# A planned kernel for attention and a squared-ReLU layer: late waits priced in the plan, and the first batch's weights made fourfold by TensorE

## The chip, the cores and the metric

The kernel runs on one core of a Trainium2 chip. The metric is the device time of one execution in microseconds (us). Engine names are those of the profile: PE is TensorE's matmuls, PEld its weight loads, DVE VectorE, ACT ScalarE, POOL GpSimd, SP the engine whose queue issues every DMA here.

## The reference

```python
def _attn_ref(x, inducing):            # x: 4 x 12480 x 128, inducing: 32 x 128
    scale = 1.0 / np.sqrt(C)
    def mab(q, kv):
        s = scale * (q @ kv.transpose(0, 2, 1))
        s = s - s.max(-1, keepdims=True)
        a = np.exp(s)
        a /= a.sum(-1, keepdims=True) + 1e-09
        return a @ kv
    h = mab(I, x)                      # 32 induced points a batch, over all 12480 tokens
    return mab(x, h)
def _moe_ref(x, w_in, w_out, s, b):    # x: 49920 x 128, w_in: 128 x 2048, w_out: 2048 x 128
    h = x @ w_in
    r = np.maximum(h, 0.0)
    g = s * (r * r) + b
    return g @ w_out
```

All of it is float32, but w_in and w_out, which come as float64. The layer runs on the attention's output.

## The kernel before

**What the bulk is.** A token's attention over 32 points and the layer's first product are folded into one: the 32 points' hT (channels by points) times w_in gives 32 x 2048 numbers, and a token's row of h is its 32 softmax weights times these. The product is taken at the fast float32r rate with both operands as a rounded high half and a low rest, so the contraction has 128 rows: `wst` holds the 32 rows four times (two copies of the high half in partitions 0 to 63, two of the low half in 64 to 127), and `a2t` holds the softmax weights as high, low, high, low. The layer's second product is split in the same way (`w_hi`, `w_lo`, and g1 with the rest g2).

Tokens go in blocks of 480, 26 blocks a batch, 104 in all. A block has 8 *pairs* (832 in all); a pair makes 256 of the 2048 rows of h by 2 matmuls (line 857), its ReLU on ACT or DVE (872, 874), its square on ACT (940) and the product h*r on DVE (895), the difference on POOL or DVE (917), and 6 matmuls into the block's output bank (965). The first NATIVE = 6 pairs are *native*: square on ACT (897) or DVE (899), and plain float32 matmuls with the unsplit `w_out_raw` (tile `wst` in line 965's rows). At a block's end line 973 or 975 adds the bias and SP writes the block out.

**Side work.** The attention of later batches runs as *visits* in the second output bank between a block's end and the next: `attend` (scores of 4 blocks against hT, a softmax on DVE and ACT, then `spread`: 4 DMAs a block write `a2t`), `scores`, `top`, `values`, `points` and `w_unit` (hT times w_in in 4 column groups, a high and a low half in `hl`, then `spread_w`: 4 DMAs for each of 4 quarters write `wst`).

**The opening.** The first batch has its own code. SP loads in the order of ORDER: x as channels by tokens in 7 groups of 4 blocks (13 pieces of 480 KB; groups 0 to 6), w_in and w_out as 64-bit words in 4 slices of 512 KB each, and x with tokens in partitions (`xQ`, pieces of 480 KB) for the groups in TURNED; the other groups are turned by PE transposes (line 428) and copies. `narrow` makes a slice float32 with 5 DVE and 2 ACT instructions (lines 307 to 324), `split_w_out` its halves (332, 334). `p1_unit` takes a group's scores (455), maximum, exp, transposes (475) and the sum of values (486); `h_unit`, `h_sums` and `h_out` join the groups into hT (line 575). Then `w_unit(0)` and `spread_w` make `wst`, and `attend_first` (line 779 to the copy into `a2t`) makes the first block's weights without DMAs; `attend(0, 0)` gives those of blocks 1 to 3. `keep_warm` fills PE with idle matmuls (1085) until the first `a2t` is there.

**What sets the order.** `Plan` runs all this as generators before anything is sent to the chip: each `yield` names an engine (or a choice of two), an estimated length and the events that it needs, and `Plan.run` is a list scheduler that emits the instruction whose (start time + WEIGHT x urgency) is least, with a filler rule (SLIP). Its output is the fixed order of each engine's instructions; the engines then wait for semaphores as the data demand. In the version before, every step that follows another becomes ready LAT = 0.1855 us after it, on whichever engine. `landing` estimates when a DMA ends.

Of the kernel before, what the change touches and what calls it, by code (L numbers as in the profile page):

```python
# [33 lines left out]
SLIP = 0.1677  # L34
WEIGHT = 0.0292
LEAN = {"ACT": -0.62, "DVE": -0.2727}
R_LEAN = {"DVE": -0.2236, "ACT": -0.2367}
# [4 lines left out]
SQ = 1.0679  # L42
MM = 0.2134
S_U = -1.7495
C_U = -10.3238
OUT_HI = 3.0192
# [3 lines left out]
SPREAD = -50.0  # L50
# [34 lines left out]
class Plan:  # L85
# [7 lines left out]
    def __init__(self):  # L93
        self.free, self.events, self.units, self.end, self.start = {}, {}, [], 0.0, 0.0

    def spawn(self, unit, urgency=0.0, ready=0.0):
        self._step(unit, urgency, ready)

    def _step(self, unit, urgency, ready=None):
        want = next(unit, None)  # L100
        if ready is None:
            ready = self.end + LAT
        if want is not None:
            eng, us, *waits = want
            if not isinstance(eng, dict):
                engs, lean = {eng: us}, LEAN
            elif isinstance(us, dict):
                engs, lean = eng, us
            else:
                engs, lean, waits = eng, LEAN, [us, *waits]  # L110
            more = sum(w for w in waits if isinstance(w, float))
            waits = [w for w in waits if not isinstance(w, float)]
            self.units.append((unit, urgency + more, ready, engs, waits, urgency, lean))
# [6 lines left out]
    def backlog(self, eng):  # L120

        ev = self.events
        return sum(u[3][eng] for u in self.units if eng in u[3] and u[2] <= self.end and all(w in ev for w in u[4]))

    def set(self, name):
        self.events[name] = self.end

    def run(self):
        ev = self.events
        while self.units:  # L130
            able = {}
            for u in self.units:
                _, urgency, ready, engs, waits, _, lean = u
                if any(w not in ev for w in waits):
                    continue
                ready = max([ready] + [ev[w] + LAT for w in waits])
                at, eng = min(
                    ((max(ready, self.free.get(e, 0.0)), e) for e in engs),
                    key=lambda x: x[0] + engs[x[1]] + lean.get(x[1], 0.0),
                )  # L140
# [12 lines left out]
            self._step(u[0], u[5])  # L153
# [3 lines left out]
def tile_attn_relu2(ctx: ExitStack, tc: tile.TileContext, xT, xN, xQ, indT, w_in, w_out, s_rep, b_rep, outT):  # L157
# [142 lines left out]
    def narrow(name, dst, *waits):  # L300
# [10 lines left out]
        yield "ACT", 0.5  # L311
        nc.scalar.activation(out=e, in_=e, func=AF.Relu, scale=8.0, bias=rebias)
        yield "ACT", 0.52
# [14 lines left out]
    def split_w_out(c):  # L328
        raw = w_out_raw
        sl = slice(c * (WC // P), (c + 1) * (WC // P))  # L330
        yield "ACT", 0.5, ("w_out", c)
        nc.scalar.copy(out=w_hi[:, sl, :], in_=raw[:, sl, :])
        yield "DVE", 0.6
        nc.vector.tensor_tensor(  # L334
            out=w_lo[:, sl, :], in0=raw[:, sl, :], in1=w_hi[:, sl, :].bitcast(F32), op=ALU.subtract
        )
        plan.set(("w_split", c))

    def bias_unit(ps, *waits):
# [9 lines left out]
        yield "ACT", 0.3  # L349
        sums = p2.tile([P, P], F32, name="s2", bufs=1)  # L350
        nc.scalar.activation(out=sums, in_=ps[:, 0:P], func=AF.Copy, scale=1.0 / M)
        yield "PE", 0.3
        nc.tensor.matmul(ps[:, 256:258], sums, ones[:, 0:2], start=True, stop=True)
        yield "DVE", 0.1
# [57 lines left out]
    def load_turned(g):  # L412
        for h in range(-(-blocks_in(g) // SB)):
            j = g * GR // SB + h
            yield "SP", 0.45, ("v done", j - 4)
            nc.sync.dma_start(out=home["q"][j % 4], in_=xQ[j])
            plan.events["turn", j] = landing(1.25)

    def turn_x(g, h, ps, *waits):

        j = g * GR // SB + h
        yield "PE", 0.87, *waits, ("x half", j), ("v done", j - 4)
# [7 lines left out]
        yield dict(ACT=0.9, DVE=1.14), 0.0  # L430
# [3 lines left out]
    def p1_unit(g, ps, *waits):  # L434
# [22 lines left out]
        yield "DVE", 0.69  # L457
# [3 lines left out]
        yield "DVE", 0.08  # L461
# [3 lines left out]
        yield "ACT", 0.75, *e_free  # L465
# [7 lines left out]
        yield "PE", 0.45  # L473
# [4 lines left out]
        yield dict(ACT=0.49, DVE=0.61), 0.0, *e_free  # L478
# [16 lines left out]
        yield dict(ACT=0.18, DVE=0.21), 0.0  # L495
# [3 lines left out]
    def common_max(m, ps):  # L499

        yield "PE", 0.07
        nc.tensor.transpose(ps[0:1, 0:P], m, ident)
        yield "DVE", 0.2
        r = sm.tile([1, 1, M], F32, name="mrow")
        nc.vector.reduce_max(out=r[:, 0, :], in_=ps[0:1, 0:P].rearrange("p (q i) -> p i q", q=NQ), axis=AX.X)
        yield "ACT", 0.25
        rq = sm.tile([1, NQ, M], F32, name="mrows", bufs=1)
        nc.scalar.mul(rq, r[:, 0:1, :].broadcast_to([1, NQ, M]), -scale)
        yield "PE", 0.11
        nc.tensor.matmul(ps[:, 128:129], rq.rearrange("p q i -> p (q i)"), ones[0:1, 0:1], start=True, stop=True)  # L510
        yield "DVE", 0.15

    def h_unit(b, ps, *waits):
        d = st[b]
        yield "DVE", 0.1, *waits
# [6 lines left out]
        yield "ACT", 0.2  # L522
# [19 lines left out]
    def h_sums(b, l, ps):  # L542

        d = st[b]
        yield "PE", 0.2
        ps = ps()
        nc.tensor.matmul(ps[:, 0:1], sel, l, start=True, stop=True)
        yield "DVE", 0.16
        rl = sm.tile([P, 1], F32, name="rl")
        nc.vector.tensor_scalar_add(rl, ps[:, 0:1], 1e-9)  # L550
        yield "DVE", 0.16
# [4 lines left out]
    def h_out(b, ps, *waits):  # L556
# [11 lines left out]
        yield "DVE", 0.35, ("rl", b)  # L568
        hg = p2.tile([P, P], F32, name="s2", bufs=1)
        nc.vector.tensor_scalar(out=hg, in0=ps[:, 0:P], scalar1=d["rl"], scalar2=None, op0=ALU.mult)  # L570
        yield "PE", 0.25
        nc.tensor.matmul(ps[:, 256:256 + P], hg, sel, start=True, stop=True)
        yield "DVE", 0.22
# [3 lines left out]
        plan.set(("hT", b))  # L577

    def w_unit(b, ps, *waits):
# [4 lines left out]
        yield "PE", 1.08, ("hT", b), *[("w_in", c) for c in range(nc_)], *waits  # L584
# [7 lines left out]
        yield dict(ACT=0.59, DVE=0.7), 0.0, *free  # L592
# [3 lines left out]
        yield "DVE", 0.7  # L596
        nc.vector.tensor_sub(out=hl[:, 1], in0=ps, in1=hl[:, 0].bitcast(F32))
        left = list(range(nc_))
        for c in range(nc_):
            plan.spawn(spread_w(b, c, hl, n, left), SPREAD + c, plan.end + LAT)  # L600

    def spread_w(b, c, hl, n, left):
        yield "SP", 2.4 if b else 1.6
# [9 lines left out]
        plan.events["wst", b, c] = landing(0.8) if b else landing(0.3, 1.7)  # L613
# [4 lines left out]
    def scores(b, g, ps, *waits):  # L618
# [15 lines left out]
        yield "PE", 1.04, ("x", b, g, 1), *waits  # L634
# [5 lines left out]
        yield "DVE", 0.65  # L640
        nc.vector.reduce_max(out=d["mx"][0:rows, g:g + 1], in_=ps[0:rows, 0:BLK], axis=AX.X)
        yield dict(ACT=0.56, DVE=0.65), 0.0
# [3 lines left out]
    def top(b, ps, *waits):  # L646

        d = st[b]
        yield "DVE", 0.16, *[("scores", b, g) for g in range(NG)], *waits
# [9 lines left out]
    def values(b, g0, ps, *waits):  # L659
# [4 lines left out]
        for g in gs:  # L664
            rows = M * blocks_in(g)
            e = d["s"][0:rows, g]
            yield "ACT", 0.8, ("top", b), *waits
# [4 lines left out]
            yield "DVE", 0.66, *e_free  # L672
# [4 lines left out]
        yield "PE", 0.1 + 0.83 * len(gs), *[("xn", b, g, half) for g in gs for half in range(-(-TB // TH))], *waits  # L677
# [13 lines left out]
        yield "DVE", 0.29  # L691
# [7 lines left out]
    def points(b, ps, *waits):  # L699

        d = st[b]
        yield "DVE", 0.16, *[("p1", b, g) for g in range(NG)], *waits
# [3 lines left out]
        yield "PE", 0.11  # L706
        nc.tensor.matmul(ps[:, 0:1], sel, l, start=True, stop=True)
        yield "DVE", 0.15
        rl = sm.tile([P, 1], F32, name="rl")
        nc.vector.tensor_scalar_add(rl, ps[:, 0:1], 1e-9)  # L710
        yield "DVE", 0.16
        nc.vector.reciprocal(out=rl, in_=rl)
        yield "ACT", 0.35
        hg = p2.tile([P, P], F32, name="s2", bufs=1)
        nc.scalar.mul(hg, d["acc"], rl)
        yield "PE", 0.25
        nc.tensor.matmul(ps[:, 256:256 + P], hg, sel, start=True, stop=True)
        yield "DVE", 0.28
# [8 lines left out]
    def attend(b, g, ps, *waits):  # L727
        nb = blocks_in(g)
        rows = M * nb
        yield "PE", 1.04, ("hT", b), ("x", b, g, 2), *waits  # L730
# [34 lines left out]
        yield "DVE", 0.66  # L765
# [4 lines left out]
        for q in mine:  # L770
            plan.spawn(spread(b, g, q), SPREAD, plan.end + LAT)

    def attend_first(ps):
# [10 lines left out]
        yield "DVE", 0.28  # L784
        mx = sm.tile([P, TB], F32, name="mx2")[0:T, 0:NQ]
        nc.vector.reduce_max(out=mx, in_=v, axis=AX.X)
        yield "DVE", 0.28
        nc.vector.tensor_tensor(out=v, in0=v, in1=mx.unsqueeze(2).broadcast_to([T, NQ, M]), op=ALU.subtract)
        yield "ACT", 0.28
        nc.scalar.activation(out=v, in_=v, func=AF.Exp, scale=scale)  # L790
        yield "DVE", 0.28
        nc.vector.reduce_sum(out=sums, in_=v, axis=AX.X)
        yield "DVE", 0.16
        nc.vector.tensor_scalar_add(sums, sums, 1e-9)
        yield "DVE", 0.18
        l = sm.tile([P, TB], F32, name="l2")[0:T, 0:NQ]
        nc.vector.reciprocal(out=l, in_=sums)
        yield "DVE", 0.28
        nc.vector.tensor_tensor(out=v, in0=v, in1=l.unsqueeze(2).broadcast_to([T, NQ, M]), op=ALU.mult)
        yield dict(ACT=0.38, DVE=0.43), 0.0  # L800
# [4 lines left out]
        yield "DVE", 0.43  # L805
        nc.vector.tensor_tensor(out=A[:, :, :, 1, :], in0=vr, in1=A[:, :, :, 0, :].bitcast(F32), op=ALU.subtract)
        n, free = ring_in_order("a2t", 3)
        yield "PE", 0.5
# [3 lines left out]
        yield dict(ACT=0.57, DVE=0.66), 0.0, *free  # L812
# [7 lines left out]
    def spread(b, g, q):  # L820

        turn, free = ring_in_order("a2t", 3)
        yield "SP", 2.4 if b or g else 1.6, *free, ("hl", b, g)
# [22 lines left out]
    def pair(k):  # L846
# [4 lines left out]
        yield "PE", 2 * MM, M_U, free, ("a2t", b, blk), ("wst", b, 2 * pr * P // WC), ("mm1", k - 1)  # L851
# [32 lines left out]
        else:  # L884
            q["R"].append((n, plan.end))
            if len(q["R"]) == 1:
                plan.spawn(square(k - n), k + SQ, plan.end + LAT)
# [18 lines left out]
        if kind == "N":  # L906
            ops = [(w_out_raw[:, 2 * pr + u, :], g[:, u, :]) for u in range(2)]
            plan.spawn(out_part(k, ops, 1.6, "w_out", lambda: plan.set(("g", g_turn))), k + OUT, plan.end + LAT)
# [12 lines left out]
        plan.spawn(out_part(k, ops, 2 * MM, "w_split", lambda: plan.set(("g2", n2))), k + OUT, plan.end + LAT)  # L921
# [6 lines left out]
    def square(k0):  # L928
# [3 lines left out]
        done = [n for n, us in q["R"] if us + LAT <= plan.start + 0.01]  # L932
# [8 lines left out]
        for i in range(lo, hi):  # L941
# [4 lines left out]
                out_part(k0 + i, ops, 4 * MM, "w_split", lambda: g1_used(q)), k0 + i + OUT_HI, plan.end + LAT  # L946
            )
        if q["R"]:
            plan.spawn(square(k0), k0 + 1 + SQ, q["R"][0][1] + LAT)
# [99 lines left out]
    def w_work():  # L1049
        yield from w_unit(0, lambda: hs[1][:, 0])  # L1050
        plan.set(("h", 1))
        plan.set(("h", 2))

    def opening():
# [17 lines left out]
        for at, f, args in loads:  # L1072
            yield from f([("ob", at - 1)] if at else [], *args)
# [20 lines left out]
    def after():  # L1094
# [4 lines left out]
        plan.spawn(w_work(), FIRST + W_URGENCY)  # L1099
# [52 lines left out]
```

## Time and profile before

| | |
|---|---|
| median of 3 runs | 1579.77 us (1578.29 to 1580.2) |
| the profiled execution's own time | 1579.85 us |
| its span | 1578.1 us |
| PE, DVE, ACT, POOL busy | 1559.3, 1462.8, 1504.9, 1479.3 us |
| granted TensorE clock, mean | 0.998 |
| DMA | 132.17 MB, mean 84 GB/s |

The span is what the trace covers from its first instruction to its last; the profiled execution's own time is 1.8 us longer. Matmuls are pipelined, so PE's busy time includes overlap, and a stretch in which PE is shown as busy throughout may still hold short stalls. A row's "idle before" is the time that an engine did nothing just ahead of those instructions, with what ended it.

### The profile page before, as it was taken

To read this page: it belongs to the slowest core of one execution; us is meant where nothing else is said; L and a number is where in the kernel's file an instruction comes from. 1 tells how busy PE (TensorE), PEld (TensorE's weight loads), DVE (VectorE), ACT (ScalarE), POOL (GpSimd) and SP (SyncE) were. 2 spreads that over 40 slices of the span, in tenths; PEclk is the share of its full clock that TensorE was granted. 3 is DMA by queue.
4 is the path that set the end of the run, shared out by engine and by line. 5 is a ranking of instruction groups with operands and counts; after the bars stand their busy time and mean duration, and the time that the engine had idled before them with its cause. 6 is when DMAs were issued, how large, how long until landed. Compare 5 with 4: busy or idle time off the path is not lost.

```text
span 1578.1 us, 24618 instructions
## 1 busy us (share of the span) xinstructions
PE 1559.3 (99%) x8140; PEld 1288.6 (82%) x8140; DVE 1462.8 (93%) x1580; ACT 1504.9 (95%) x1780; POOL 1479.3 (94%) x668
## 2 busy tenths in 40 slices
PE   8799999999999999999999999999999999999999
PEld 5478888888888888888788788888888888888887
DVE  5899999999999989999999999999999999999997
ACT  5799999999999999999999999999999999999998
POOL 0299999999999999999999999999999999999998
PEclk9999999999999999999999999999999999999999
DMA  9332224212133233221223322322222112112110
GB/s 319 97 113 87 90 88 150 64 51 90 38 107 119 73 122 119 73 73 56 76 66 101 111 78 100 120 82 63 79 59 66 39 51 70 32 51 70 53 33 23
DMA packets 54522, 132.17 MB, mean 84 GB/s; under 512 B 11548, under 2 KB 38044, under 8 KB 54396
## 3 DMA queue, kind: packets, MB, share of 16 engines
q1 hardware_dynamic: 54396, 130.59, 26.1%
q8 instruction: 66, 1.08, 0.3%
q14 instruction: 60, 0.49, 0.1%
HBM read 75.48 MB, written 25.56 MB: 64 GB/s over the span
## 4 chain that ended last, share of the span: by engine, by line
PE 96%; DVE 1%; DMA 1%; SPq 1%; ACT 0%; issue 0%; ACTq 0%; DVEq 0%
PE x L965 67%; PE h L857 23%; PE x L735 2%; PE x L683 1%; PE x L638 1%; DMA xn<-in_xQ_dram 1%; PE h L428 0%; SPq L606 0%; DVE w_lo L334 0%; PE x L486 0%; DMA wst<-hl 0%; DMA xt<-in_xT_dram 0%; PE x L588 0%; PE x L455 0%; DVE g L895 0%
## 5 line engine op out<-in xcount | busy, mean ns | idle before, releaser
L917 POOL TENSOR_TENSOR g<-g,g 128x960 fp32r<-128x960 f32 x660 | 1478.1, 2286 | 93.3 <-ACT g L940 73.3
L965 PE MATMUL x<-g,w_hi 128*128 128x480 f32 x3304 | 1062.1, 375 | 0.0
L940 ACT ACTIVATE g<-r 128x960 fp32r<-128x960 f32 (+1 forms) x812 | 796.6, 1020 | 16.2 <-DVE r L874 5.1
L895 DVE SCALAR_TENSOR_TENSOR g<-h,r 128x960 f32<-128x960 f32 x660 | 743.4, 1147 | 34.7 <-ACT r L872 26.8
L965 PEld LDWEIGHTS x<-g,w_hi 128*128 128x128 f32 x3304 | 618.2, 187 | 88.4 <-POOL g L917 1.7
L872 ACT ACTIVATE r<-h 128x960 f32<-128x960 f32 x673 | 634.3, 968 | 19.3 <-PE h L857 14.6
L965 PE MATMUL x<-g,w_lo 128*128 128x480 f32 x1652 | 619.8, 375 | 2.9 <-DVE w_lo L334 2.9
L857 PE MATMUL h<-a2t,wst 128*128 128x480 f32 x1664 | 500.3, 382 | 5.1 <-DMA wst<-hl 4.1
L857 PEld LDWEIGHTS h<-a2t,wst 128*128 128x128 f32 x1664 | 300.1, 187 | 97.9 <-issue 38.9
L965 PEld LDWEIGHTS x<-g,w_lo 128*128 128x128 f32 x1652 | 309.6, 187 | 51.9 <-issue 5.5
L917 DVE TENSOR_TENSOR g<-h,g 128x960 fp32r<-128x960 f32 x166 | 191.6, 1154 | 17.6 <-ACT g L940 8.1
L895 DVE SCALAR_TENSOR_TENSOR h<-h,r 128x960 f32<-128x960 f32 x166 | 192.2, 1158 | 6.6 <-ACT r L872 6.3
L874 DVE TENSOR_SCALAR r<-h 128x960 f32<-128x960 f32 x159 | 182.9, 1150 | 9.3 <-PE h L857 7.7
L973 ACT ACTIVATE ob<-x,bias,s_sb 128x480 f32<-128x480 f32 x101 | 75.6, 749 | 10.8 <-PE x L965 10.2
L735 PE MATMUL x<-xt,hT 128*32 128x480 f32 x208 | 28.3, 578 | 0.0
L766 DVE TENSOR_TENSOR hl<-x,hl 128x480 fp32r<-128x480 f32 (+1 forms) x28 | 18.4, 657 | 8.1 <-ACT hl L188 7.2
L638 PE MATMUL x<-xt,ind_sb 128*32 128x480 f32 x156 | 21.2, 578 | 0.0
L741 DVE STREAM_TRANSPOSE x<-x 128x480 f32<-128x480 f32 (+1 forms) x28 | 19.3, 689 | 1.5 <-PE x L735 1.4
L683 PE MATMUL x<-xn,eT 128*32 128x128 f32 (+1 forms) x630 | 20.7, 274 | 0.0
L683 PEld LDWEIGHTS x<-xn,eT 128*32 128x32 f32 (+1 forms) x630 | 17.5, 109 | 3.9 <-issue 2.3
L759 DVE STREAM_TRANSPOSE x<-x 128x480 f32<-128x480 f32 (+1 forms) x28 | 19.5, 697 | 1.0
L750 DVE TENSOR_REDUCE x<-x 128x15 f32<-128x480 f32 (+1 forms) x28 | 18.4, 659 | 1.4 <-ACT x L748 1.0
(149 smaller groups left out, 368.7 us busy)
## 6 DMA issues: line engine op xcount, KB each, us to landing
xt<-in_xT_dram SPq DMA_DIRECT2D x41, 960.0 KB, 5.1
out_dram<-ob SPq DMA_DIRECT2D x104, 240.0 KB, 2.0
a2t<-hl SPq DMA_DIRECT2D x412, 60.0 KB, 2.0
xn<-in_xN_dram SPq DMA_DIRECT2D x18, 512.0 KB, 4.7
xn<-in_xN_dram SPq DMA_DIRECT2D x18, 448.0 KB, 5.7
xt<-in_xT_dram SPq DMA_DIRECT2D x13, 480.0 KB, 4.3
wst<-hl SPq DMA_DIRECT2D x64, 64.0 KB, 2.0
r<-in_xT_dram SPq DMA_DIRECT2D x7, 480.0 KB, 8.8
```

The lines of the kernel that those rows point to most:

```text
L638: nc.tensor.matmul(ps[M * q:M * (q + 1), 0:BLK], ind_sb, xt[:, q], start=True, stop=True)
L683: nc.tensor.matmul(ps[M * c:M * (c + 1), 0:P], eT[0:rows, n], xn_tiles[b, g, half][0][0:rows, n - half * TH], start=m < P // M, stop=m + P ...
L735: nc.tensor.matmul(ps[M * q:M * (q + 1), 0:BLK], hT[:, 0:M], xt[:, q], start=True, stop=True)
L759: nc.vector.transpose(out=s, in_=s)
L857: nc.tensor.matmul(h[:, u, 0:BLK], wst[:, c * P:(c + 1) * P], A, start=True, stop=True)
L872: nc.scalar.activation(out=r, in_=hv, func=AF.Relu)
L874: nc.vector.tensor_scalar(out=r, in0=hv, scalar1=0.0, scalar2=None, op0=ALU.max)
L895: nc.vector.scalar_tensor_tensor(out=g, in0=hv, scalar=0.0, in1=r, op0=ALU.max, op1=ALU.mult)
L917: eng.tensor_tensor(out=g2, in0=g, in1=hi.bitcast(F32), op=ALU.subtract)
L940: nc.scalar.activation(out=q["g1_t"][:, sl, :], in_=q["r_t"][:, sl, :], func=AF.Square)
L965: nc.tensor.matmul(o, w, g, start=first and n == 0, stop=left == 0 and n == len(ops) - 1)
L973: nc.scalar.activation(out=ob, in_=o, func=AF.Identity, bias=bias, scale=s_sb)
```

## The change

- **The plan's prices.** A step's delay after the one that releases it now depends on both engines: none on PE, 0.15 us on DVE, 0.175 on ACT when the same engine did the earlier step, else LAT plus the waker's share (0.1 for PE, 0.03 DVE, 0.015 ACT, 0.03 POOL). Nearly all estimated lengths are replaced (a DVE step of a visit 0.57 instead of 0.65, PE's visits about 0.1 longer). Eleven or so urgencies and SLIP, WEIGHT move, most a little.
- **Fourfold weights.** `w_first` takes the place of `w_unit(0)` and its DMAs: hT has its 32 columns four times already, so 4 full float32 matmuls (128 columns of weights, 512 columns each) give all four copies at once; a copy rounds them into `wst`, and a DVE subtraction turns partitions 64 to 127 into the low rest.
- **The opening's loads.** Group 4 is turned by PE too (TURNED is 5 alone: two pieces of xQ fewer); two slices of w_out move ahead of x 2 and x 4, the order of w_in moves; a row of `xQ` in HBM is 48 floats (192 bytes) longer.
- **Later loads wait.** The x loads that stand ahead of block 0 (for the first visits) are planned after the `a2t` of block 1 has landed instead of at once.
- NATIVE is 5; a pair's first matmuls no longer name the pair before as an event (their order stays: a pair is spawned by the one before).

The core of the diff (lengths alone left out):

```diff
 LAT = 0.1855
-SLIP = 0.1677
-WEIGHT = 0.0292
+WAKE = {"PE": 0.1, "DVE": 0.03, "ACT": 0.015, "Pool": 0.03, "SP": 0.0}
+SAME = {"PE": 0.0, "DVE": 0.15, "ACT": 0.175, "Pool": 0.1, "SP": 0.0}
+SLIP = 0.1757
+WEIGHT = 0.0234
-R_LEAN = {"DVE": -0.2236, "ACT": -0.2367}
+R_LEAN = {"DVE": -0.2236, "ACT": -0.2106}
-SQ = 1.0679
+SQ = 1.3068
-S_U = -1.7495
+S_U = -2.6693
-OUT_HI = 3.0192
+OUT_HI = 3.1
-SPLIT_U = 11.22
-NATIVE = 6
-H_U = -5.8
-N_U = -2.41
-W_IN_U = -200.15
-W_OUT_U = 0.21
+SPLIT_U = 9.84
+NATIVE = 5
+H_U = -73.92
+N_U = -0.27
+W_IN_U = -194.01
+W_OUT_U = 0.92
+W_STEP = 1.0
-TURNED = (4, 5)
+TURNED = (5,)
+Q_PAD = 48
 ORDER = (
-    ("x", 0), ("x", 1), ("w_in", 0), ("x", 2), ("x", 3), ("w_in", 1), ("x", 4), ("w_in", 2), ("x", 5),
-    ("w_in", 3), ("x", 6), ("q", 4), ("q", 5), ("w_out", 0), ("w_out", 1), ("w_out", 2), ("w_out", 3),
+    ("x", 0), ("x", 1), ("w_out", 0), ("x", 2), ("w_in", 0), ("x", 3), ("w_out", 1), ("x", 4), ("w_in", 1),
+    ("w_in", 2), ("x", 5), ("x", 6), ("w_in", 3), ("q", 5), ("w_out", 2), ("w_out", 3),
 )
...
+    def lag(self, src, e):
+        return SAME[e] if src == e else LAT + WAKE[e]
+    def ready(self, u):
...
+        return {
+            e: max([at + self.lag(src, e) if at else 0.0] + [ev[w] + self.lag(self.by.get(w), e) for w in u[4]])
+            for e in u[3]
+        }
...
-            nc.sync.dma_start(out=home["q"][j % 4], in_=xQ[j])
-            plan.events["turn", j] = landing(1.25)
+            nc.sync.dma_start(out=home["q"][j % 4], in_=xQ[j, :, 0:SB * NQ * P])
+            plan.events["turn", j] = landing(2.1)
...
+    def w_first(c, ps, done):
+        yield "PE", 0.95, ("hT", 0), ("w_in", c)
...
+        sl = slice(c * WC, (c + 1) * WC)
+        ps = ps()
+        nc.tensor.matmul(ps, d["hT"], w_in_sb[:, sl], start=True, stop=True)
+        yield dict(ACT=0.48, DVE=0.6), 0.0
+        copy(d["wst"][:, sl], ps)
+        yield "DVE", 0.6
+        lo = d["wst"][P // 2:P, sl]
+        nc.vector.tensor_sub(out=lo, in0=ps[P // 2:P], in1=lo.bitcast(F32))
+        plan.set(("wst", 0, c))
...
-        yield "PE", 2 * MM, M_U, free, ("a2t", b, blk), ("wst", b, 2 * pr * P // WC), ("mm1", k - 1)
+        yield "PE", 2 * MM, M_U, free, ("a2t", b, blk), ("wst", b, 2 * pr * P // WC)
...
-            yield from f([("ob", at - 1)] if at else [], *args)
+            yield from f([("ob", at - 1) if at else ("a2t", 0, 1)], *args)
...
-        plan.spawn(w_work(), FIRST + W_URGENCY)
+        for c in range(F // WC):
+            plan.spawn(w_work(c), FIRST + W_URGENCY + W_STEP * c)
```

More of the change, by code (lines that the diff above doesn't have):

```diff
@@ L112, in _step @@
             waits = [w for w in waits if not isinstance(w, float)]
-            self.units.append((unit, urgency + more, ready, engs, waits, urgency, lean))
+            self.units.append([unit, urgency + more, (ready, src), engs, waits, urgency, lean, None])
     def extend(self, us):
@@ L118, in extend @@
         self.free[self.eng] = self.end
-    def backlog(self, eng):
-        ev = self.events
-        return sum(u[3][eng] for u in self.units if eng in u[3] and u[2] <= self.end and all(w in ev for w in u[4]))
     def set(self, name):
         self.events[name] = self.end
+        self.by[name] = self.eng
+    def lag(self, src, e):
+        return SAME[e] if src == e else LAT + WAKE[e]
+    def ready(self, u):
+        ev, (at, src) = self.events, u[2]
+        for w in u[4]:
+            if w not in ev:
+                return None
+        return {
+            e: max([at + self.lag(src, e) if at else 0.0] + [ev[w] + self.lag(self.by.get(w), e) for w in u[4]])
+            for e in u[3]
+        }
     def run(self):
-        ev = self.events
         while self.units:
@@ L132, in run @@
             for u in self.units:
-                _, urgency, ready, engs, waits, _, lean = u
-                if any(w not in ev for w in waits):
+                if u[7] is None:
+                    u[7] = self.ready(u)
+                if u[7] is None:
                     continue
-                ready = max([ready] + [ev[w] + LAT for w in waits])
+                urgency, engs, lean = u[1], u[3], u[6]
                 at, eng = min(
-                    ((max(ready, self.free.get(e, 0.0)), e) for e in engs),
+                    ((max(at, self.free.get(e, 0.0)), e) for e, at in u[7].items()),
                     key=lambda x: x[0] + engs[x[1]] + lean.get(x[1], 0.0),
@@ L429, in turn_x @@
         x_used(g, h)
-        yield dict(ACT=0.9, DVE=1.14), 0.0
+        yield dict(ACT=0.85, DVE=1.05), 0.0
         copy(t.rearrange("p a q c -> p a (q c)"), ps[0:T])
@@ L577, in h_out @@
         plan.set(("hT", b))
+    def w_first(c, ps, done):
+        yield "PE", 0.95, ("hT", 0), ("w_in", c)
+        d = st[0]
+        if "wst" not in d:
+            d["wst"] = wst_pool.tile([P, F], F32R, name="wst")
+        sl = slice(c * WC, (c + 1) * WC)
[7 more added lines that the diff above has]
+        plan.set(("wst", 0, c))
+        for name in done:
+            plan.set(name)
     def w_unit(b, ps, *waits):
@@ L583, in w_unit @@
         nc_ = F // WC
-        yield "PE", 1.08, ("hT", b), *[("w_in", c) for c in range(nc_)], *waits
+        yield "PE", 1.19, ("hT", b), *[("w_in", c) for c in range(nc_)], *waits
         d["wst"] = wst_pool.tile([P, F], F32R, name="wst")
@@ L612, in spread_w @@
             plan.set(("hl", n))
-        plan.events["wst", b, c] = landing(0.8) if b else landing(0.3, 1.7)
+        plan.events["wst", b, c] = landing(0.8)
     def scores(b, g, ps, *waits):
@@ L648, in top @@
         d = st[b]
-        yield "DVE", 0.16, *[("scores", b, g) for g in range(NG)], *waits
+        yield "DVE", 0.09, *[("scores", b, g) for g in range(NG)], *waits
         ps = ps()
@@ L666, in values @@
             e = d["s"][0:rows, g]
-            yield "ACT", 0.8, ("top", b), *waits
+            yield "ACT", 0.68, ("top", b), *waits
             nc.scalar.activation(
@@ L676, in values @@
             eTs[g] = eT, e_turn, rows
-        yield "PE", 0.1 + 0.83 * len(gs), *[("xn", b, g, half) for g in gs for half in range(-(-TB // TH))], *waits
+        yield "PE", 0.19 + 0.9 * len(gs), *[("xn", b, g, half) for g in gs for half in range(-(-TB // TH))], *waits
         ps = ps()
@@ L701, in points @@
         d = st[b]
-        yield "DVE", 0.16, *[("p1", b, g) for g in range(NG)], *waits
+        yield "DVE", 0.09, *[("p1", b, g) for g in range(NG)], *waits
         ps = ps()
@@ L886, in pair @@
             if len(q["R"]) == 1:
-                plan.spawn(square(k - n), k + SQ, plan.end + LAT)
+                plan.spawn(square(k - n), k + SQ, plan.end)
             yield "DVE", 1.065, S_U
@@ L931, in square @@
         yield "ACT", 0.893, *([] if "g1_t" in q else [q["g1"][1]])
-        done = [n for n, us in q["R"] if us + LAT <= plan.start + 0.01]
+        done = [n for n, us in q["R"] if us + LAT <= plan.start + 0.02]
         lo, hi = done[0], done[-1] + 1
@@ L1047, in tile_attn_relu2, with w_work @@
     before = [-2, -1, *turns]
[L1049 to L1052, printed above, removed]
+    def w_work(c):
+        yield from w_first(c, lambda: hs[1 + c // 2][:, c % 2], [("h", 1 + c // 2)] if c % 2 else [])
     def opening():
```

164 lines of the change are left out of this document (83 added, 81 removed).

## The prediction

> **What bounds the kernel now.** I read the page first (busy times, chain), then how many matmuls fall into a stretch, then the opening by stages, by the chain and by the waits. The page:
>
> ```profile
> span 1578.1 us, 24618 instructions
> PE 1559.3 (99%) x8140; PEld 1288.6 (82%) x8140; DVE 1462.8 (93%) x1580; ACT 1504.9 (95%) x1780; POOL 1479.3 (94%) x668
> PE 96%; DVE 1%; DMA 1%; SPq 1%; ACT 0%; issue 0%; ACTq 0%; DVEq 0%
> ```
>
> PE is the bound, and the chain that ended last is PE for 96%. Since a busy PE can hide stalls, I count. First the pace: two timeline rows of PE with 29 matmuls of 480 columns from the one's start to the other's; a native product; two visits.
>
> ```profile
> 299.76 0.59 PE L857 MATMUL h<-a2t,wst 128*128 128x480 f32 x2
> 305.95 0.37 PE L965 MATMUL x<-g,w_hi 128*128 128x480 f32 x1
> ...
> 60.57 1.77 PE L965 MATMUL x<-g,wst 128*128 128x480 f32 x4
> ...
> 80.04 1.01 PE L638 MATMUL x<-xt,ind_sb 128*32 128x480 f32 x8
> ...
> 235.06 1.94 PE L683 MATMUL x<-xn,eT 128*32 128x128 f32 x60
> ```
>
> (305.95 - 299.76) / 29 = 0.213 us a matmul; a native pair's 4 stand 0.40 apart (1.77 less one of 0.57, by 3), so 1.6 us; a visit of 8 takes 1.0, one of 60 takes 1.9. Then the counts of line 965 and, below, line 857, before and after 100 us:
>
> ```profile
> 49.50:100.00 50.50, 31.02 (x107) 20.03 (x108) 1.00 0.38 118
> 100.00:1574.00 1474.00, 1171.47 (x4874) 911.23 (x4873) 1.00 0.24 77
> ...
> 49.50:100.00 50.50, 15.46 (x50) 8.56 (x50) 1.00 0.38 118
> 100.00:1574.00 1474.00, 484.85 (x1614) 291.59 (x1614) 1.00 0.24 77
> ```
>
> From 100 us on: 6488 matmuls x 0.2134 = 1384.5 us, and by the code 46 visits of `attend` and `scores` x 1.0, values worth 10.5 x 1.9 and some 6 of small matmuls: about 72. That leaves some 17 us of 1474 in which PE stalls (1.1%). From 49.5 to 100: 24 native matmuls x 0.40, 133 others x 0.213, and 2.5 of side work make 40.5 of 50.5 us, a loss of about 10. Before 49.5 PE does no pair at all. So the time is: start of the first pair, plus 1498 us of work that no part of the change but NATIVE touches, plus about 27 us of stalls, plus 4 at the end. The change can gain in the first and in the stalls. The opening by stages (PE, PEld, DVE, ACT, POOL busy, granted clock, DMA share and GB/s):
>
> ```profile
> 20.00:30.00 10.00, 8.00 (x109) 4.46 (x106) 8.99 (x21) 7.95 (x18) 0.00 (x0) 1.00 0.98 304
> 30.00:40.00 10.00, 8.63 (x97) 6.62 (x97) 3.16 (x11) 3.65 (x9) 0.00 (x0) 0.66 0.89 278
> ...
> 45.00:50.00 5.00, 4.21 (x26) 2.67 (x26) 4.93 (x13) 2.63 (x6) 0.00 (x0) 1.00 0.29 70
> 50.00:60.00 10.00, 5.92 (x20) 3.13 (x18) 9.86 (x18) 9.94 (x13) 0.00 (x0) 1.00 0.75 218
> ```
>
> To 40 us it is DMA (share 0.9 to 1.0) while DVE and ACT have room; from 45 to 60 DVE is full. The chain names the transfer:
>
> ```profile
> 23.83 7.92 DMA xn<-in_xQ_dram
> ...
> 31.79 1.92 PE x L486 x28
> ...
> 34.84 1.89 PE h L428 x8
> ...
> 38.81 1.02 PE h L486 x16
> ...
> 42.57 0.20 DVE hT L575
> ...
> 55.57 4.37 DMA wst<-hl
> ```
>
> **The change, part by part.**
>
> *A. When hT is ready.* What ends last is `xQ`. Its four issues and their times to landing, and the DMA rate with x and weights in the queue (first row) and with `xQ` in it (second):
>
> ```profile
> L416 SPq DMA_DIRECT2D xn<-in_xQ_dram x4: 325/338/402, 23.3 to 26.2; - x4
> DMA to landing us min/median/max: 6.3/8.0/9.7
> ...
> 12.00:22.00 10.00, 8.90 (x123) 6.35 (x121) 7.28 (x15) 7.72 (x17) 0.00 (x0) 1.00 1.03 416
> 26.00:34.00 8.00, 5.69 (x56) 2.91 (x49) 6.06 (x14) 4.93 (x13) 0.00 (x0) 0.84 1.01 241
> ```
>
> They land from 29.6 (23.3 + 6.3) to 35.9 (26.2 + 9.7), 2.1 us apart, at 241 GB/s against 416 for the rest. After: two pieces fewer are -4.2; two slices of w_out now stand ahead, 524 kB each at 416 GB/s, +2.5. The last piece lands at 34.2. What follows it before is 6.9 us, to 42.77; of that, group 6's turn (1.89) and its values (1.02) need no longer wait behind group 4's `xQ` and are done earlier. From the end of line 486 at 39.8 to hT it is 3.0; before that come group 5's values, between 1.0 (full clock) and 1.9 (these rows, at half): 4.0 to 4.9, I take 4.5, so hT at 38.7, **4.0 us earlier**. Bounds: nothing earlier than 2 (group 4's transposes, two turning copies and part of two narrowed slices now fall into 20 to 30, where DVE has 10% left) and 6 if the longer rows of `xQ` load at the other pieces' pace, 1.2 instead of 2.1, twice.
>
> The Trainium skill's "DMA: Bandwidth & Descriptors", section "Latency and other measured facts", has that padding a large row pitch by 192 B did not restore the rate while 4 KiB did; that pitch was 4 MiB, and nothing here shows this one. Its section on why a DMA increments its semaphore by 16 lets 120 rows use only 15 engines, padded or not. By both the pieces stay at 2.1 and the sum as it is; with a pad that works it would be 1.7 less.
>
> *B. From hT to the first pair.* Before it is 49.57 - 42.77 = 6.8 us:
>
> ```profile
> 45.53 0.69 DVE L597 TENSOR_TENSOR hl<-h,hl 128x512 fp32r<-128x512 f32 x1
> ...
> 47.62 0.53 PE L811 MATMUL x<-accb,hl 120*128 120x120 f32 x4 [0.79 <-DVE hl L806]
> 48.19 0.56 ACT L188 CAST a2t<-x 128x480 fp32r<-128x480 f32 x1 [1.14 <-PE x L811]
> 49.57 1.13 PE L857 MATMUL h<-a2t,wst 128*128 128x480 f32 x4
> ```
>
> That is `attend_first`, which stays. `w_first` is 4 float32 products of 512 columns: by the native row (0.40 a pass of 480, two passes) 0.86 each, 3.4 us of PE, in time that idle matmuls fill now. It has 4 copies instead of one (about 0.6 on ACT) and 4 subtractions instead of one, 4 x 0.69: +2.1 on DVE. Against that, half of w_out's narrowing (5 DVE instructions of 512 columns a slice, at most 0.69 each by line 597's row, so 5 to 7 us for two slices, an estimate) leaves the full stretch for the time before 40. The first quarter of `wst` is ready some 1.0 + 0.9 + 0.6 + 0.7 and 0.6 of hand-overs after hT, 3.8, less than 6.8. So B stays: 0, between -1 and +1.2. The 16 `wst` DMAs go; what is late next is the `a2t` copy at 48.75. If that cover went, line 857 would wait on the later quarters, 0.9 us apart.
>
> *C. Stalls up to 100 us*, about 10 now. The rows that name them, with the subtractions of `split_w_out` and the two ACT steps of a native pair:
>
> ```profile
> PE h L857 <- DMA wst<-hl: 4.1, 2, 2.7
> PE x L965 <- DVE w_lo L334: 2.9, 1, 2.9
> ...
> 59.57 0.68 DVE L334 TENSOR_TENSOR w_lo<-wst,w_hi 128x512 fp32r<-128x512 f32 x1
> ...
> 67.97 5.58 DVE L334 TENSOR_TENSOR w_lo<-wst,w_hi 128x512 fp32r<-128x512 f32 x3 [0.40 <-ACT w_hi L332]
> ...
> L872 ACT ACTIVATE r<-h 128x960 f32<-128x960 f32 x10 | 9.5, 961 | 2.2 <-PE h L857 2.2
> L897 ACT ACTIVATE g<-r 128x960 f32<-128x960 f32 x5 | 4.9, 1004 | 0.1
> ```
>
> Of the 4.1 the shorter wait, 1.4, falls where PE has no product ready anyway (pair 0's square is not done), so 2.7 goes. The `w_lo` stall of 2.9 stands behind three subtractions that took 1.9 each on average beside POOL's first work, where the first, at 59.57 with POOL idle, took 0.68; with two slices narrowed, and so split, before the pairs begin I let 2.0 go. Late next is ACT: a native pair costs it 0.96 + 1.00 (lines 872, 897) against 2.03 on PE, and narrowing and splitting come on top; 0.5 lost. Sum **-4.2**, bounds -1 (DVE still has the softmax of `attend(0, 0)`, splits and two slices to do, and sets the pace) and -7 (both named waits go whole). The loads that wait have the other block writes behind them on SP and the visits from block 1 or 2 on waiting for them; a block is 64 matmuls x 0.213 = 13.7 us, so they have that long to land. Nothing lost.
>
> *D. NATIVE 5:* 4 x 0.40 = 1.6 of PE become 6 x 0.213 = 1.28: **-0.3**.
>
> *E. The order from 100 us on.* Weight loads of line 857 that came late, 100 to 1574, and a pair's first product behind one (0.67, while those at 299.76 took 0.59):
>
> ```profile
> PEld h L857 <- issue: 34.1, 71, 0.8
> PEld h L857 <- DVE g L895: 10.2, 33, 0.8
> PEld h L857 <- DVE r L874: 3.9, 5, 0.8
> ...
> 76.89 0.67 PE L857 MATMUL h<-a2t,wst 128*128 128x480 f32 x2
> ```
>
> 109 late loads x 0.08 = 9 of the 17 us. The new plan charges PE 0.1 after any other engine's step, so where another product is ready it is put first. The trace of before can't show the new order. Bounds: -9 (all go) and +9 (as many new ones, from shorter visit steps that make the plan promise more than DVE keeps); I take a quarter of the gain, **-2.5**, since the order was already within 1.1% of the work.
>
> Sum: -4.0 + 0 - 4.2 - 0.3 - 2.5 = -11.0 us against the profiled execution's 1579.85 (span and 1.8 around it), 0.08 above the median of the runs: 1568.8.
>
> **The rivals.**
>
> 1. *The start moves, the stalls don't go:* DVE has the same work between hT and the first `a2t` of block 1 and only shifts. For it: DVE at 99% from 45 to 60. Against it: 5 to 7 us of narrowing leave, 2.1 come. A and D alone: 1575.5.
> 2. *The clock.* The 30 to 40 row has 0.66, after a stretch in which PE waited for `xQ`. If it is at half for `w_first`, its 3.4 us become 6.9 and `attend_first`'s transposes stand behind them on PE: up to 3.4 later, 1572.3. Against it: group 4's wait is gone, and PE has idle matmuls to run from the last group on. The Trainium skill's "TensorE: Matmul & The Clock Gate", Part 1, says that PE drops to half after an idle window of about 3.4 us and needs as long a busy one to return. By that rule the wait for the last `xQ` piece is just such a window; the 0.66 agrees.
> 3. *The order is much better:* stalls after 100 us halve, -8 instead of -2.5: 1563.3.
> 4. *Slower: the order is worse.* The place is line 857 behind 895 and 872: with visit steps planned 0.08 shorter, DVE's h*r comes later than planned and PE waits. A loses nothing, but stalls from 100 us on must grow by 8.5 + 3.2 = 11.7, from 17 to 29, for the kernel to be slower by 0.2%; doubled to 34 it gives 1579.85 - 8.5 + 17 = 1588.4. Against it: the order is within 1.1% of the work already with one price for every wait, and PE's own wait, which decides, becomes dearer in the plan.
> 5. *The change does not do what it says:* the planner lets DVE take the two early w_out slices ahead of the turning copies, SP waits for a buffer of theirs with x 5, x 6 and `xQ` queued behind, and hT is not earlier; only C, D, E remain: 1572.8.
>
> **How the numbers follow.** The forecast with A to E near their middle has 0.50, rival 1 0.13, 2 0.09, 3 0.15, 4 0.07, 5 0.06. The likeliest one's own range is 1563 to 1574, from A's and C's bounds. The range goes to 1559 below (rival 3 with A at 6) and 1576.5 above (rival 1). A measurement of this kernel tells about 0.2%, 3.2 us, from no change. Faster by more (under 1576.6): the forecast, 2, 3, 5 and most of 1, 0.89; within it: the rest of 1 and some of 4, 0.06; slower: 0.05.
>
> **What would show it.** A: line 575 at 38 to 40 us and the two `xQ` pieces 2.1 apart. B: line 857 first at 44 to 47, no `wst` DMA before the second batch, 4 products of `w_first` 0.9 apart (1.8 if rival 2 holds). C: the waits on `wst` gone, that on `w_lo` under 1. E: 71 + 33 + 5 late loads down by a quarter. The prediction is wrong if hT is as late as before, or if line 965's count from 100 to 1550 us is lower than now.

## The result, and the profile after

| | before | changed |
|---|---|---|
| median of 4 runs | 1579.99 us (1578.29 to 1582.64) | 1571.53 us (1570.15 to 1573.63) |
| profiled execution, its own time | 1579.85 | 1570.15 |
| its span | 1578.1 | 1568.4 |

The ratio is 0.9946, 95% interval 0.9928 to 0.9964: 8.5 us faster where 11.0 were forecast. The page of the changed kernel (PE still sets the time), then the opening by stages as before:

```profile
span 1568.4 us, 24582 instructions
PE 1555.2 (99%) x8154; PEld 1293.2 (82%) x8154; DVE 1479.8 (94%) x1609; ACT 1488.3 (95%) x1741; POOL 1482.4 (95%) x670
...
20.00:30.00 10.00, 9.17 (x124) 5.96 (x124) 9.03 (x21) 9.81 (x18) 0.00 (x0) 1.00 0.90 338
30.00:40.00 10.00, 8.32 (x125) 6.39 (x123) 8.51 (x25) 6.71 (x17) 0.00 (x0) 1.00 0.58 163
...
45.00:50.00 5.00, 3.65 (x22) 1.83 (x21) 4.45 (x9) 4.29 (x9) 0.00 (x0) 1.00 0.00 0
50.00:60.00 10.00, 9.96 (x49) 5.38 (x51) 9.79 (x16) 10.00 (x14) 0.00 (x0) 1.00 0.06 14
```

From 50 to 60 PE is busy 9.96 instead of 5.92, no DMA of weights is left there, and in this execution the clock does not fall between 30 and 40. The chain around hT, and the first pair (line 857 is 887 now, 965 is 995, 334 is 346, 895 is 925):

```profile
27.74 7.49 DMA xn<-in_xQ_dram
35.28 1.07 PE x L498 x28
...
36.66 1.02 PE h L498 x16
...
40.20 0.61 PE h L1113 x3
...
40.24 0.29 DVE L587 COPY hT<-h 128x128 f32<-128x128 f32 x1
...
47.80 0.69 PE L887 MATMUL h<-a2t,wst 128*128 128x480 f32 x2 [0.28 <-ACT a2t L200]
```

hT is there at 40.53 instead of 42.77, the first pair at 47.80 instead of 49.57. The counts of lines 995 and, below, 887:

```profile
47.80:100.00 52.20, 35.37 (x128) 23.71 (x128) 1.00 0.30 100
100.00:1564.00 1464.00, 1154.32 (x4853) 908.41 (x4852) 1.00 0.25 77
...
47.80:100.00 52.20, 17.75 (x57) 10.29 (x58) 1.00 0.30 100
100.00:1564.00 1464.00, 465.28 (x1608) 293.27 (x1607) 1.00 0.25 77
```

By the prediction's own count: up to 100 there are 20 native passes x 0.40, 165 others x 0.213 and some 4 of side work (one visit of 8 more than before falls ahead of 100), 47 of 52.2, a loss of 5 where there were 9 to 10. From 100 on it is 6461 x 0.2134 + 71 = 1450 of 1464, so 14 us of stalls where there were 17. So the profiled 9.7 us are about 1.8 of an earlier start, 4 to 5 of early stalls, 0.3 of NATIVE and 3 to 4 of later stalls.

### The profile page after: what moved, and what is told of

It reads as the page before. It is cut to its first block, busy times and chain, and to the rows that moved or that the text cites. A ratio compares the mean times of both kernels' runs of the same rounds, so it can differ in the third digit from the quotient of the medians.

```text
span 1568.4 us, 24582 instructions
## 1 busy us (share of the span) xinstructions
PE 1555.2 (99%) x8154; PEld 1293.2 (82%) x8154; DVE 1479.8 (94%) x1609; ACT 1488.3 (95%) x1741; POOL 1482.4 (95%) x670
## 4 chain that ended last, share of the span: by engine, by line
PE 93%; DVE 2%; DMA 2%; ACT 1%; issue 1%; POOL 1%; SPq 0%; POOLq 0%; ACTq 0%; DVEq 0%
PE x L995 66%; PE h L887 23%; PE x L765 2%; PE x L713 1%; PE x L668 1%; DMA g<-in_w_out_dram 1%; DVE g L925 1%; POOL g L947 1%; DMA xn<-in_xQ_dram 0%; DMA xt<-in_xT_dram 0%; ACT g L970 0%; POOLq L1180 0%; ACT r L902 0%; PE x L618 0%; SPq L858 0%
## 5 line engine op out<-in xcount | busy, mean ns | idle before, releaser
L995 PE MATMUL x<-g,w_hi 128*128 128x480 f32 x3308 | 1042.1, 376 | 0.2 <-POOL g L947 0.2
L902 ACT ACTIVATE r<-h 128x960 f32<-128x960 f32 x654 | 614.7, 967 | 27.7 <-PE h L887 24.7
L887 PE MATMUL h<-a2t,wst 128*128 128x480 f32 x1664 | 483.0, 381 | 2.9 <-DVE g L925 2.6
L887 PEld LDWEIGHTS h<-a2t,wst 128*128 128x128 f32 x1664 | 303.6, 188 | 83.7 <-issue 28.7
L904 DVE TENSOR_SCALAR r<-h 128x960 f32<-128x960 f32 x178 | 204.8, 1150 | 11.6 <-PE h L887 9.5
L947 DVE TENSOR_TENSOR g<-h,g 128x960 fp32r<-128x960 f32 x165 | 190.5, 1154 | 11.7 <-ACT g L970 1.0
L765 PE MATMUL x<-xt,hT 128*32 128x480 f32 x208 | 28.3, 578 | 0.0
L787 DVE TENSOR_TENSOR x<-x,l 128x480 f32<-128x480 f32 (+1 forms) x28 | 18.6, 665 | 0.9
L776 DVE TENSOR_TENSOR x<-x,mx 128x480 f32<-128x480 f32 (+1 forms) x28 | 18.4, 656 | 0.1
```

The costliest lines, as they stand in the source:

```text
L765: nc.tensor.matmul(ps[M * q:M * (q + 1), 0:BLK], hT[:, 0:M], xt[:, q], start=True, stop=True)
L887: nc.tensor.matmul(h[:, u, 0:BLK], wst[:, c * P:(c + 1) * P], A, start=True, stop=True)
L902: nc.scalar.activation(out=r, in_=hv, func=AF.Relu)
L904: nc.vector.tensor_scalar(out=r, in0=hv, scalar1=0.0, scalar2=None, op0=ALU.max)
L947: eng.tensor_tensor(out=g2, in0=g, in1=hi.bitcast(F32), op=ALU.subtract)
L995: nc.tensor.matmul(o, w, g, start=first and n == 0, stop=left == 0 and n == len(ops) - 1)
```

## The experiments

Each run's ratio is to the kernel before on the same chip, with its 95% interval. Stalls are measured more finely here, as the sum of what two neighbouring matmuls of the pairs stand apart beyond their pace (a stall beside a visit is not in it). From the first pair to 100 us ("early") it is 9.9 us before and 4.7 changed, after 100 us 15.7 and 11.6. Executions with the same order on every engine agree after 100 us to 0.1; their early stalls differ with the clock, from 4.7 where it stays full to 6.7 where it falls to half twice. The loads, the prices and the lengths were not tried one by one in the kernel before with urgencies of their own, so what each run shows is what a part is worth beside the others.

**The changed kernel again (a0).** 

> The changed kernel once more, beside the others on the same chip. Both theories: 1571.5, between 1569.5 and 1573.5, ratio to the kernel before 0.9935 to 0.996.

1570.83 us, 0.9946 (0.9934 to 0.9959). As expected; the runs below are set against it.

**The weights by DMA again.** The core of the edit (`w_work` is `w_unit(0)` again; `spread_w` has the first batch's length and landing time of before):

```diff
+    def w_work():
+        yield from w_unit(0, lambda: hs[1][:, 0])
...
-        for c in range(F // WC):
-            plan.spawn(w_work(c), FIRST + W_URGENCY + W_STEP * c)
+        plan.spawn(w_work(), FIRST + W_URGENCY)
```

> The changed kernel with the first batch's weights spread by 16 DMAs again. Theory (the DMAs cost because the pairs wait for the last quarters): first pair at 47 to 48.5 as in the changed kernel, a wait on wst of 2.5 to 4 us in the first 20 us of pairs, 1574 to 1576. Rival (the plan has enough other work there and DVE sets the pace, so the DMAs' wait only takes the place of another): 1570 to 1573.

1572.09 us, 0.9949 (0.9937 to 0.9961): not to be told from a0. The wait itself is back, as the theory had it (waits, 46 to 60 us):

```profile
PE h L887 <- DMA wst<-hl: 3.3, 3, 1.5
```

Yet the time hardly moves: early stalls are 7.5 against 6.2 in a0's trace, and the clock is at half for 6.8 us from 51 on here, for 3.4 in a0. Those after 100 us are 14.0 against 11.6, and nothing says that this difference is due to the DMAs. The rival holds as far as the time goes: when the wait on `wst` is gone, others take most of its place, and in the changed kernel the fourfold weights are worth at most 1 to 2 us.

**The fourfold weights alone, in the kernel before.** `w_first` in place of `w_unit(0)`, nothing else.

> The kernel before with the first batch's weights made fourfold by TensorE alone. Theory (in the kernel before the DMAs waited for hl, stood behind an x load in SP's queue and cost 4.1 us of PE waits): 2.5 to 4 us faster, 1575.5 to 1577.5, no wait on wst. Rival (another wait takes its place, as with the DMAs put back into the changed kernel): within 1.5 us of before.

1577.59 us, 0.9981 (0.9973 to 0.9990), 2.6 us faster, at the edge of the theory's range. No wait on `wst` is left; early stalls fall from 9.9 to 6.0. The first pair comes 1.5 later (51.06): 0.6 of it is a later hT (43.38), the other 0.9 fits DVE's four subtractions, which stand in `attend_first`'s way. The order after 100 us is no better (15.5 us). So this part is worth some 2.6 us there, and 1 to 2.5 between executions with the same mean clock.

**One price for every hand-over.**

```diff
-WAKE = {"PE": 0.1, "DVE": 0.03, "ACT": 0.015, "Pool": 0.03, "SP": 0.0}
-SAME = {"PE": 0.0, "DVE": 0.15, "ACT": 0.175, "Pool": 0.1, "SP": 0.0}
+WAKE = dict.fromkeys(("PE", "DVE", "ACT", "Pool", "SP"), 0.0)
+SAME = dict.fromkeys(("PE", "DVE", "ACT", "Pool", "SP"), LAT)
```

> The changed kernel with one price of 0.1855 us for every hand-over, all lengths new. Theory (the dearer wait of PE removed the late weight loads): late loads of a pair's first product after 100 us back from 72 to 100 or more, 3 to 5 us slower, 1574 to 1577. Rival (the new lengths did it): 1570 to 1573, late loads as now.

1593.4 us, 1.0092 (1.0076 to 1.0109): the late loads are back as the theory had it, but the time is far worse than its range, and slower than the kernel before. (The share that `lag` adds, 0.1 us for PE, is that of the engine that waits, not of the one that wakes it.) Late weight loads from 100 us on, of the changed kernel and of this one:

```profile
PEld h L887 <- issue: 22.5, 48, 0.8
PEld h L887 <- DVE g L925: 7.0, 18, 1.0
PEld h L887 <- DVE r L904: 4.7, 6, 0.8
```

```profile
PEld h L887 <- issue: 29.6, 83, 1.5
PEld h L887 <- DVE g L925: 18.7, 50, 1.4
PEld x L995 <- issue: 16.8, 26, 0.8
```

Stalls after 100 us are 28.3, early ones 12.6, and the first pair comes at 50.86. So the new lengths without the price of a wait make a far worse plan; that it promises products before they are there fits these rows, but the plan's own times were not compared.

**The prices alone, in the kernel before.** `Plan` with WAKE and SAME; old lengths and opening.

> The kernel before with the two tables of hand-over prices (and what they need in the planner) alone; old lengths, urgencies and opening. After the run with one price for all, theory (prices and lengths belong together: the old, longer lengths already held part of a wait's cost): the order from 100 us on is not better than before, 1577 to 1584, PE stalls after 100 us 15 to 20 us. Rival (the prices alone make the better order): stalls after 100 us fall to 12 or less, 1574 to 1577.

1584.43 us, 1.0029 (1.0019 to 1.0039), just above the range; stalls after 100 us are 22.2, above it too. The theory's point holds: neither half works alone here. (The urgencies fit one or the other whole plan, so neither run says anything of prices or lengths by themselves with urgencies of their own.)

**An order drawn anew.** WEIGHT 0.0236 instead of 0.0234.

> The changed kernel with WEIGHT 0.0236 instead of 0.0234, which means nothing by itself: how far the time moves with an order drawn anew under the same prices. Theory (part of the gain after 100 us is this one order's): stalls after 100 us 13 to 15 us instead of 11.6, 1572 to 1575. Rival (the prices carry it, any such order has it): 11 to 12.5, 1570 to 1572.

1570.7 us, 0.9941 (0.9928 to 0.9955), stalls after 100 us 11.1: the rival. The orders of PE, DVE and ACT differ in some 70 to 120 places each, and the gain stays: as far as one new order tells, it belongs to the plan's settings together (prices, lengths, urgencies). Not to every such plan, though: with other changes of the opening they were 14.0 (weights by DMA), 13.8 (old loads) and 14.5 (split early).

**The loads of before.** ORDER and TURNED of the kernel before.

> The changed kernel with the loads of the kernel before: its order, and groups 4 and 5 from xQ. Theory (the load order brought hT 2 us earlier and took w_out's narrowing out of the full stretch): hT at 42 to 43.5, first pair 2 to 3 later, w_lo wait back, 1573.5 to 1577. Rival (the first pair hangs on attend_first and DVE, not on hT): hT later, total 1570 to 1573.

1577.7 us, 0.9985 (0.9976 to 0.9994), 6 to 7 us slower than a0 and slightly beyond the range. hT is at 44.1, the first pair at 51.4, and the wait for `w_lo` is 1.6 (1.0 with the new order). Against a0's trace some 4 of it are the start, 1.3 early stalls, 2 the later order. The clock has a part in it: here it is at half from 31.2 to 38, as in the kernel before, and the eleven executions have a mean clock of 0.994 to 0.997 where a0's have 0.998 and 0.999. In the kernel before, executions at 0.996 take 3 us more than those at 0.999 (medians 1581.9 and 1578.9), so by an estimate some 3 of the 7 us come with the clock. With the rest of the change in place, the loads are its largest part; the new loads alone in the kernel before were not run.

**The later loads at once.**

```diff
-            yield from f([("ob", at - 1) if at else ("a2t", 0, 1)], *args)
+            yield from f([("ob", at - 1)] if at else [], *args)
```

> The changed kernel with the x loads ahead of block 0 planned at once. Theory (no DMA of the weights is left that they could delay, and the a2t of block 1 is wanted only at 67): the same, 1570 to 1573. Rival (1.9 MB ahead of the a2t copies in the queues delays block 1): a2t lands 4 us or more later and the pairs of block 1 wait for it, 1574 to 1576.

1570.64 us, 0.9945 (0.9931 to 0.9959): the same. That the loads wait is worth nothing here.

**Rows of xQ not padded (pad0, Q_PAD 0 instead of 48), and 128 rows instead of 120 (q128).** Every engine's order is that of the changed kernel. The edit of q128:

```diff
-        home["q"] = [t[0:T].rearrange("p n c -> p (n c)") for t in xn]
+        home["q"] = [t.rearrange("p n c -> p (n c)") for t in xn]
...
-                ((0, 0), (0, 0), (0, Q_PAD)),
+                ((0, 0), (0, P - T), (0, Q_PAD)),
```

> The changed kernel with rows of xQ not padded; the order of every engine is the same. Theory (120 rows load slowly whether padded or not): last xQ piece lands within 0.7 us of the changed kernel's (33.6 to 35.2), the same time, 1570 to 1573. Rival (the pad did speed them): last piece 1.5 us or more later, 1572 to 1574.

> The changed kernel with 128 rows a piece of xQ (8 rows of zeros below the 120) into the same tiles, so 6.7% more bytes; the order of every engine is the same. Theory (120 rows don't spread over all DMA engines as 128 do): the two pieces land 1.2 to 1.5 us apart instead of 2.0 to 3.6, the last 1 to 2 us earlier, hT and the first pair with it, 1569 to 1571. Rival (something else slows them, as their place in HBM): as late as now or later, 1571 to 1573.

1571.36 us, 0.9938 (0.9926 to 0.9950), and 1569.35 us, 0.9931 (0.9918 to 0.9944). The two pieces' times to landing, changed kernel, pad0, q128:

```profile
DMA to landing us min/median/max: 4.5/6.0/7.5
```

```profile
DMA to landing us min/median/max: 4.4/5.9/7.4
```

```profile
DMA to landing us min/median/max: 3.7/4.1/4.5
```

The pad does nothing, as the prediction took it. The Trainium skill's "DMA: Bandwidth & Descriptors", section "Latency and other measured facts", had the same of 192 B at a far larger pitch. With 128 rows the two land 1.24 us apart, the last at 31.8 instead of 35.2, although more bytes move; in the 20 gaps between 120-row pieces of the other traces the least is 1.98. One trace doesn't settle it, though: in the next run, with 128 rows again, they land 3.7 apart. The Trainium skill's "DMA: Bandwidth & Descriptors", section "Why a DMA increments its semaphore by 16 and not by 1", gives 120 rows 15 engines, which would explain 7%, an estimate. What else a 120-row piece loses stays open.

The time gains some 2 us on pad0 of the same chip, and the intervals overlap: hT is at 39.55, 7.8 us behind the last piece, since DVE is full with narrowing that the plan had put ahead of it.

**128 rows, and the plan told so.** `landing(1.3)` instead of `landing(2.1)`.

> The 128-row xQ with the plan told of it (a piece lands in 1.3 us instead of 2.1). Theory (in the 128-row run hT came only 0.3 to 1.0 us earlier because DVE still did narrowing that the plan had put ahead of the late piece): hT 0.5 to 1.5 us earlier than there (39.55), 1567.5 to 1569.5 if stalls after 100 us stay at 11 to 12. Rival (an order drawn anew loses as much after 100 us as the opening gains): stalls 13 or more, 1570 to 1573.

1570.74 us, 0.9937 (0.9923 to 0.9950). hT at 39.19 and the first pair at 46.47, 0.4 earlier than in q128; stalls after 100 us 11.7. Both expectations miss: hT gains less than 0.5, the stalls don't grow, and the time is no better than q128's. Nor is the loading: the pieces land at 29.8 and 33.5 here.

```profile
DMA to landing us min/median/max: 3.5/5.2/6.8
```

q128 remains the fastest run, but neither is shown to beat the changed kernel.

**The split before POOL.** SPLIT_U -100 instead of 9.84.

> The changed kernel with the split of w_out urgent (SPLIT_U -100 instead of 9.84), so that its subtractions are done before POOL starts. Theory (DVE's subtractions run 2.3 us each beside POOL and hold up the product that PE waits for at 65): no w_lo subtraction over 1 us, the stall of 2.0 at 65 gone, 1567.5 to 1570. Rival (the split then delays attend_first's DVE steps and the first pair instead): first pair 1 to 2 us later, 1570 to 1573.

1572.98 us, 0.9953 (0.9941 to 0.9966). The subtractions of `split_w_out`, changed kernel and this one:

```profile
L346 DVE TENSOR_TENSOR w_lo<-wst,w_hi x4: 670/1319/2745, 34.7 to 63.3; 128x512 fp32r<-128x512 f32 x4
```

```profile
L346 DVE TENSOR_TENSOR w_lo<-wst,w_hi x4: 681/681/692, 34.1 to 59.3; 128x512 fp32r<-128x512 f32 x4
```

All four take 0.68 and the stall at 65 us is gone, as the theory had it, but the time misses its range. It lies in the rival's, and not for the rival's reason: the first pair is not later (47.6). Early stalls are 4.4, hardly less than the 4.7 of the changed kernel's profiled execution, and the order after 100 us comes out with 14.5 us of stalls, which costs more than was gained.

## Why the prediction was right

The measured 1571.5 lies in the likeliest case's own range; the steps fare as follows.

- **A, hT 4.0 earlier: 2.2** in the profiled execution, 2.3 to 3.4 in pad0, a0 and loads_early, whose engines have the same order. This is the mis-sized term. In the profiled execution the last piece landed at 35.2, not 34.2, and 5.3 instead of 4.5 us followed, with group 6's values (1.02 in the chain) still behind the late piece. SP's issue of `xQ` waits for group 3's values, which now come later, and the DMA queue ran short meanwhile (the row's share is 0.71, 0.99 before):

```profile
26.00:30.00 4.00, 4.00 (x60) 2.51 (x60) 3.81 (x9) 3.96 (x8) 0.00 (x0) 1.00 0.71 227
...
27.23 1.43 SPq L428 DMA_DIRECT2D xn<-in_xQ_dram  x2
```

  Yet the landing is not all. In a0 the last piece landed at 33.6, ahead of the forecast, and hT came at 39.84, 6.2 us behind it. There the chain to hT does not go through `xQ`: it goes through DVE, whose maxima, narrowing and split the new order of loads moved into this stretch (8.51 of the 10 us from 30 to 40 instead of 3.16). From a0's chain:

```profile
33.33 0.60 DVE w_in_sb L336
33.93 0.60 DVE wst L336
34.53 0.07 DVE nmall L533
34.60 0.60 DVE w_lo L346
...
35.97 1.02 PE h L498 x16
```

  So the step that failed is that hT follows the last `xQ` piece by 4.5 us: DVE's work ahead of hT ends about as late as the loads, and the sum put that at nothing, though the lower bound of 2 named it. Bounds of 2 to 6 held. That a piece follows the other by about 2 us, padded or not, held in a0 (2.0); in the profiled execution it was 3.6.
- **B, no change: 0.5 later.** Right within its bounds; `wst`'s first quarter was not the last. The late step before line 887 is `attend_first`'s copy, behind DVE's new subtractions.
- **C, -4.2: about -4 to -5.** Right in size. The `wst` waits went; the `w_lo` wait fell from 2.9 to 1.0 in PE, and a new one of 2.0 came for DVE's h*r behind the two subtractions slowed by POOL:

```profile
PE h L887 <- DVE g L925: 2.0, 1, 2.0
PE x L995 <- DVE w_lo L346: 1.0, 1, 1.0
...
L346 DVE TENSOR_TENSOR w_lo<-wst,w_hi 128x512 fp32r<-128x512 f32 x2 | 4.6, 2350 | 0.0
```

  No single part carries this: in the kernel before the fourfold weights alone took early stalls from 9.9 to 6.0, and in the changed kernel taking out either them or the new loads gives back only 1.3. The larger part of the loads' worth (6 to 7 us, against at most 2.6 for the weights) is in the start.
- **E, -2.5: -3 to -4.** The three rows of late loads went from 109 to 72, a third instead of a quarter.
- **Rivals 1, 3 and 5** did not come: the early stalls went, the later ones fell by 3 to 4 and not by 8, and hT is earlier. SP does wait 4.0 us for a buffer of narrowing (line 331) with x 5, x 6 and `xQ` queued behind, as rival 5 had it, but the queue stays full meanwhile (share 1.02 from 12 to 22).
- **Rival 2, the clock,** did not show in the changed kernel's profiled execution, but it does occur. In the profiled one of the run with WEIGHT moved (1574.31; its fastest, 1568.33, had the clock at 1.000) the clock was at half for 6.8 us around hT:

```profile
38.00:42.00 4.00, 3.45 (x27) 2.46 (x24) 2.62 (x7) 1.50 (x3) 0.00 (x0) 0.50 0.00 0
...
51.03 0.70 PE L887 MATMUL h<-a2t,wst 128*128 128x480 f32 x2 [0.28 <-ACT a2t L200]
```

  Its first pair came at 51.0 instead of 47.8, 3.2 later where the rival gave 3.4. In other executions of the same kernel it stays away: its runs with a mean clock of 0.996 and 0.997 took 1574.9 and 1574.3, those with 1.000 took 1568.3 and 1569.9. The prediction took the wait for the last `xQ` piece as the cause. In the kernel before the clock is at half from 31.4 to 38.3, so it fell ahead of that wait, behind 3.4 us in which PE was busy for 1.74. In the run with WEIGHT moved it fell behind 3.4 us with 2.62 busy. These are the two stretches ahead of the fall:

```profile
28.00:31.40 3.40, 1.74 (x13) 0.64 (x9) 2.87 (x9) 3.12 (x8) 0.00 (x0) 1.00 1.03 242
...
33.80:37.20 3.40, 2.62 (x44) 1.92 (x46) 2.96 (x8) 2.65 (x8) 0.00 (x0) 1.00 0.78 246
```

  No single idle time of PE in them is over 1.1 us. The Trainium skill's "TensorE: Matmul & The Clock Gate", Part 1, has an idle window of about 3.4 us ahead of the fall. The falls of 3.4 and 6.8 us here agree with that length; a stretch without work does not show in these traces.

  The clock also carries a little of the gain. At a mean clock of 0.999 the executions of the kernel before have a median of 1578.9, the five of the changed kernel 1570.8: 8.1 us at the same clock, where the medians of all executions are 8.5 to 9.1 apart.
- **Rival 4, a worse order,** is what one price for all makes: 28 us of stalls after 100 us, 1593. By the rival's sum (8.5 us of gain kept, 12.6 of stalls more) that would have been 4 us more than before; it is 13, because the gain in the start and in the early stalls went too (first pair at 50.86, early stalls 12.6). The change as a whole is not that case.

## What to carry to other kernels

Lengths and hand-over prices of a plan are one set: the new lengths without a price for the late wait cost 22 us here, the price without the lengths cost 4. In this opening, which waits for loads, their order was worth more than the removal of DMAs that stood on the visible wait. Look at what fills the queue while its issuer waits, and at which engine will set the pace once the load is earlier: here it was DVE, and a still earlier `xQ` gained little. A local repair in a list-scheduled kernel must be judged by the whole run, since a new order can move the bulk by 2 to 3 us.

## What the runs showed of the hardware

A piece of 120 rows of 4096 B landed 2.0 to 3.7 us behind the one before it; with 128 rows it was 1.24 in one trace and 3.7 in another. A VectorE subtraction with both inputs in SBUF took 0.68 us alone and 2.35 on average while GpSimd's tensor instructions ran. The Trainium skill's "SBUF — State Buffer", section "Who interferes with whom", says that two such instructions contend, and these rows agree. TensorE's clock fell to half for 3.4 or 6.8 us at a time, in some executions of a kernel and not in others, behind stretches of 3.4 us in which PE was busy for 1.4 (a0, at 67.8) to 2.6 us (the run with WEIGHT moved, at 37.3).
